# RoPE attention before two MLPs: q's rotation of five head pairs summed in PSUM, and the 1e-9 of the softmax sums on the scalar engine

## The chip, the core and the metric

The kernel runs on one core of a Trainium2 chip. The metric is the device time of one execution in microseconds (us), as a median of three runs. The engines are TensorE (PE in the profile, its weight loads PEld), VectorE (DVE), ScalarE (ACT), GpSimd (POOL) and SyncE (SP, which issues the DMAs). They run side by side, each in the order of its own queue, and wait for each other by semaphores.

## What is computed

Attention with rotary positions over 4 batches x 8 heads, 576 tokens, 64 dimensions a head; then two MLPs over the 2304 tokens (512 to 2048 to 512 each). All data is float32.

```python
def rotate(x):                       # half = 32
    x1, x2 = x[..., :half], x[..., half:]
    return concatenate([x1 * cos - x2 * sin, x1 * sin + x2 * cos], -1)
scores = rotate(q) @ rotate(k).T / sqrt(D)
scores = scores - max(scores, -1)
attn = exp(scores)
attn = attn / (sum(attn, -1) + 1e-09)
x = attn @ v                         # regrouped to 2304 x 512
h = x @ w_in;  g = where(h >= 1, h, where(h <= -1, 0, (h + 1) ** 2 / 4))
x = g @ w_out
r = maximum(x @ w_in2, 0);  out = (s * r * r + b) @ w_out2
```

## The kernel before, in words

**Pairs and units.** Two heads lie on the 128 partitions, so there are 16 pairs. A pair has nine units (`UNITS`, k = 0 to 8), 144 units in all: eight score tiles of 128 query rows, and at k = 4 a tile of the remainders. The loop over units calls five steps in the order `ORDER = "qltaf"`.

- `do_qk`: the score matmuls of a unit into one of two PSUM buffers `sc` (L307), the row maximum `nm` on DVE (L309), the exponentials `p` on ACT with their row sums (L314).
- `do_load`: the preparation of the next pairs. At k = 0 the q of pair i+1 is rotated (`rope_pair`), at k = 2 its k; at k = 4 and 6 the q and k of pair i+2 are loaded. It also issues the conversions of MLP weights (`convert`: ACT L126, four DVE instructions L127 to L130, two POOL products `wm`, two POOL sums `w`, ACT L131).
- `do_t`, two units later: transposes `tp` of `p` on PE, copied to `pt` by ACT (L333) or DVE (L335). For the last unit of each of the two groups of a pair also `inverse`, the reciprocal of the row sums: 1e-9 is added on DVE (L367, and L369 for the remainder), the reciprocal is taken on DVE (L371), and POOL spreads it to a tile `eb` (L373).
- `do_av`, four units later: the products with v (L355 to L360), the transposes `rm` of `eb` (L380), and `u = av * r` on DVE (L388 to L391).
- `do_fill`, from unit 48 on: matmuls `h` and `y` of the first MLP for batches that are finished, as filling between the attention's.

**The rotation of q before.** The host's layout holds q twice, as two planes: itself, and with its halves swapped and signed. `load_qk` loads both planes into one tile (L217, 576 KB). `rope_pair` multiplies both by the table (POOL, four instructions of 128x288; DVE for pair 1, L247) and adds them on DVE (L249, 128x576). `lay_q` then splits the sum into two fp32r parts for the two heads: for each, ACT writes the rounded part (L262, 64x576) and DVE the rest (L263, 64x576).

**What sets the order.** Within the attention no order is written out by hand: each engine's order comes from a scheduler that works with its own estimates of durations, so one edit can move instructions of all engines. The buffers are: four banks of PSUM for `tp`, `tr`, `av`, `rm`, `h`, `y` together (`bank`), two for `sc` of two banks each, four tiles for the loads of q and k, two sets of `qs`, `kh` and `kz`. Behind the attention come the two MLPs, from about 455 us to the end, in a fixed order.

Of the kernel before, what the change touches and what calls it, by code (L numbers as in the profile page):

```python
# [8 lines left out]
F32 = mybir.dt.float32  # L9
F32R = mybir.dt.float32r  # L10
# [3 lines left out]
AF = mybir.ActivationFunctionType  # L14
ALU = mybir.AluOpType
# [4 lines left out]
B, H, S, D = 4, 8, 576, 64  # L20
# [3 lines left out]
P = 128  # L24
# [28 lines left out]
N2A = 288  # L53
CAV = None
BF = 0
SPLITX = 1
N1 = 288

# [2 lines left out]
def kernel(ctx, tc, qq, kk, vv, tab, ww1, ww2, s, b, out):  # L61
    nc = tc.nc
# [6 lines left out]
    const = ctx.enter_context(tc.tile_pool(name="const", bufs=1))  # L69
    ident = const.tile([P, P], F32, name="ident")  # L70
    make_identity(nc, ident)
    s_sb = const.tile([P, 1], F32, name="s_sb")
    b_sb = const.tile([P, 1], F32, name="b_sb")

    def pool_tt(out, in0, in1, op, dim=-1):

        n = out.shape[dim]
        free = 1
        for x in out.shape[1:]:
            free *= x  # L80
        k = min(n, -(-free // PW))
        for i in range(k):
            c = [slice(None)] * len(out.shape)
            c[dim] = slice(n * i // k, n * (i + 1) // k)
            c = tuple(c)
            nc.gpsimd.tensor_tensor(out=out[c], in0=in0[c], in1=in1[c], op=op)  # L86
# [13 lines left out]
    exps = {}  # L100
# [96 lines left out]
    att = pa.enter_context(tc.tile_pool(name="att", bufs=1, side="right", reuse_waits="tile"))  # L197
    att2 = pa.enter_context(tc.tile_pool(name="att2", bufs=2, side="right", reuse_waits="tile"))
    ps_s = pp.enter_context(tc.tile_pool(name="ps_s", bufs=2, space=PSUM))
    ps_b = pp.enter_context(tc.tile_pool(name="ps_b", bufs=4 - BF, space=PSUM))  # L200
    ps_f = pp.enter_context(tc.tile_pool(name="ps_f", bufs=BF, space=PSUM)) if BF else ps_b

    tab_sb = att.tile([P, 2, S], F32, name="tab_sb")

    def bank(name):
        return ps_b.tile([P, 512], F32, tag="bank", name=name)

    qk_in, v_in, stacks = {}, {}, {}

    WHOLE = [slice(0, S)]  # L210
    HALVES = [slice(0, 288), slice(288, S)]

    def load_qk(i, nm, pieces=WHOLE):
        bb, hp = divmod(i, NP)
        t = att2.tile([P, 2, S], F32, tag="qkin", name=f"{nm}in", bufs=QB)
        for c in pieces:
            nc.sync.dma_start(out=t[:, :, c], in_=(qq if nm == "q" else kk)[bb, hp, :, :, c])  # L217
        qk_in[nm, i] = t

    def load_v(i):  # L220
        bb, hp = divmod(i, NP)
        t = att2.tile([P, 5, 2, D], F32, tag="vin", name="vin", bufs=VB)
        for out, src in ((t[:, :, 1], vv[bb, hp, :, :, 1]), (t[:D, :4, 0], vv[bb, hp, D:, :4, 0]), (t[D:, :4, 0], vv[bb, hp, :D, 1:, 0]), (t[D:, 4, 0], vv[bb, hp, :D, 0, 0])):
            nc.sync.dma_start(out=out, in_=src)
        v_in[i] = t
# [9 lines left out]
    kz_t = [att.tile([P, 2, S], F32R, name=f"kz{n}") for n in range(2)]  # L235
# [5 lines left out]
    def rope_pair(i, nm, mul, add, lo_eng, pieces=WHOLE):  # L241

        t = qk_in.pop((nm, i))
        tt = {nc.gpsimd: pool_tt, nc.vector: nc.vector.tensor_tensor}
        last = None
        for c in pieces:
            tt[mul](out=t[:, :, c], in0=t[:, :, c], in1=tab_sb[:, :, c], op=ALU.mult)  # L247
            r = t[:, 1, c]
            tt[add](out=r, in0=t[:, 0, c], in1=r, op=ALU.add)  # L249
            last = (lay_q if nm == "q" else lay_k)(i, t, c, lo_eng)  # L250
        return last

    SELF = [slice(0, D), slice(D, P)]

    def lay_q(i, t, c, lo_eng):

        st = stacks["q", i] = qs_t[i % 2]
        r = t[:, 1, c]
        for j in range(2):
            own, other = SELF[j], SELF[1 - j]  # L260
            at = slice(j * QW + c.start, j * QW + c.stop)
            nc.scalar.activation(st[own, at], r[own], AF.Copy, scale=0.125)  # L262
            nc.vector.scalar_tensor_tensor(out=st[other, at], in0=r[own], scalar=0.125, in1=st[own, at], op0=ALU.mult, op1=ALU.subtract)  # L263

    def lay_k(i, t, c, lo_engs):
        if c.start == 0:
            stacks["k", i] = att.tile([P, 2, S], F32R, tag="kh", name="kh", bufs=2), kz_t[i % 2]
        kh, kz = stacks["k", i]
        tt = {nc.gpsimd: pool_tt, nc.vector: nc.vector.tensor_tensor}
        r = t[:, 1, c]  # L270
        if i > 0:
            hi, lo = t[:, 0, c].bitcast(F32R), r.bitcast(F32R)
            nc.scalar.copy(hi, r)
            pool_tt(out=lo, in0=r, in1=t[:, 0, c], op=ALU.subtract)
            for j in range(2):
                own = SELF[j]
                for rows in SELF:
                    nc.sync.dma_start(out=kh[rows, j, c].bitcast(F32), in_=t[own, 0, c])
                m = nc.sync.dma_start(out=kz[own, j, c].bitcast(F32), in_=t[own, 1, c])
            return m.ins  # L280
        for j in range(2):
            own, other = SELF[j], SELF[1 - j]
            nc.scalar.copy(kh[own, j, c], r[own])
            m = nc.sync.dma_start(out=kh[other, j, c].bitcast(F32), in_=kh[own, j, c].bitcast(F32))
            tt[lo_engs[j]](out=kz[own, j, c], in0=r[own], in1=kh[own, j, c], op=ALU.subtract)
        return m.ins
# [6 lines left out]
    def qk(i, k):  # L293
        if k == 0:
            sums_t[i] = att2.tile([P, 9], F32, tag="sums", name="sums")
        j, t = UNITS[k]
        sc = ps_s.tile([P, 2, 512], F32, tag="sc", name="sc")
        if j is None:
            places = [(0, 512), (1, S + D)]
        else:  # L300
            places = [(j, t * P + j * (QW + D))]
        straight = [[(0, 0, 288)], [(0, 288, 288)]]
        moved = [[(0, D, 288)], [(0, 352, 224), (224, 0, D)]]
        for half in range(2):
            todo = [(stacks["q", i][:, c:c + P], r[:, h], w) for h, c in places for r in stacks["k", i] for w in (moved if j is None and h == 0 else straight)[half]]
            for m, (l, r, (o, k0, n)) in enumerate(todo):
                nc.tensor.matmul(sc[:, half, o:o + n], l, r[:, k0:k0 + n], start=m == 0, stop=m == len(todo) - 1)  # L307
        nm = att.tile([P, 1], F32, tag="nm", name="nm", bufs=4)
        nc.vector.tensor_reduce(out=nm, in_=sc[:, :, :288], axis=AX.XY, op=ALU.max, negate=True)  # L309
        if j != 1:  # L310
            p_t[i, t] = att.tile([P, 2 * S], F32, tag="p", name="p", bufs=PB)
        p = p_t[i, t][:, S * (j == 0):S * (j == 0) + S]
        col = 8 if j is None else 2 * t + j
        exps[i * 9 + k] = nc.scalar.activation(p, sc[:, :, :288], AF.Exp, bias=nm, scale=1.0, accum_out=sums_t[i][:, col:col + 1]).ins  # L314
        if j is None:
            nc.scalar.copy(p_t[i, t][:, S:S + D], p[:, 512:])
# [46 lines left out]
    def inverse(i, g):  # L363

        e = att2.tile([P, 5], F32, tag="sume", name="sume")
        sm = sums_t[i]
        nc.vector.tensor_scalar_add(e[:, 0:4], sm[:, 4 * g:4 * g + 4], 1e-9)  # L367
        if g == 0:
            nc.vector.tensor_scalar_add(e[:, 4:5], sm[:, 8:9], 1e-9)  # L369
        m = 5 - g  # L370
        nc.vector.reciprocal(e[:, :m], e[:, :m])  # L371
        eb = att2.tile([P, 4, D], F32, tag="eb", name="eb")
        nc.gpsimd.tensor_copy(eb, e[:, 0:4].unsqueeze(2).to_broadcast([P, 4, D]))  # L373
        return e, eb
# [79 lines left out]
    def convert():  # L454
        while pending:
            sl = pending.pop(0)
            if sl.made < 2:
                sl.half(wst, WB)
                break
# [20 lines left out]
    def do_load(n):  # L480
        if n < len(units):
            i, k = units[n]
            if i + 1 < NPAIR:
                if k == 0:
                    rope_pair(i + 1, "q", nc.gpsimd if i else nc.vector, nc.vector, None)
                elif k == 2:
                    rope_pair(i + 1, "k", nc.gpsimd, nc.gpsimd, [nc.gpsimd, nc.vector])
                elif k == 3:
                    load_v(i + 1)
                elif k in (4, 6) and i + 2 < NPAIR:  # L490
                    load_qk(i + 2, "q" if k == 4 else "k")

        if n in range(33, 51, 2) or n in range(70, 110, 4):
            with tc.issue_after(exps[n - 14]):
                convert()
# [124 lines left out]
    last = FC * N1  # L620
# [57 lines left out]
```

## Time and profile before

| | us |
|---|---|
| median of 3 runs (1163.46 to 1164.19) | 1163.69 |
| the profiled execution, its own time | 1162.87 |
| its span in the profile | 1161.1 |
| PE busy in the span | 1100.2 (95%) |
| DVE busy | 610.5 (53%) |
| ACT busy | 690.8 (59%) |
| POOL busy | 563.6 (49%) |

The profiled execution is 0.82 us under the median, and 1.8 us of it lie outside its span. Busy shares are means over stages with different limits: up to about 143 us only attention runs, from there to about 455 us attention with the first MLP's matmuls between it, then the MLPs alone. So the rows below are read stage by stage: 14.7 us is the first row maximum, 77.3 that of the fourth pair, 143.6 that of unit 53. A "row" of a view that groups instructions gives the line in the code, the engine, the operation, output and inputs with their shapes, the count, then busy us and the mean ns of one, then the idle time of that engine ahead of them and what ended it.

### The profile page before, as it was taken

The numbers are of one execution on the slowest core, as the hardware profiler recorded it, in microseconds if no ns is written. First come the engines' busy times: TensorE is split into PE (matmuls) and PEld (weight loads), VectorE is DVE, ScalarE is ACT, GpSimd is POOL, SyncE is SP. The second block draws the span as 40 slices with busy tenths as digits, with TensorE's granted clock in tenths as the row PEclk, the third lists the DMA queues.
The fourth block names the chain that finished last, engine by engine and source line by source line (L and its number), as shares of the span: only waits on it lengthen the run. The fifth ranks groups of instructions, "written<-read, shape, count | busy, mean of one in ns | idle before, by whom it ended". The sixth has DMA issues, their size and how long they took to land.

```text
span 1161.1 us, 18714 instructions
## 1 busy us (share of the span) xinstructions
PE 1100.2 (95%) x6720; PEld 993.9 (86%) x6720; DVE 610.5 (53%) x1030; ACT 690.8 (59%) x1450; POOL 563.6 (49%) x748
## 2 busy tenths in 40 slices
PE   4887899899999999999999899999999999999998
PEld 4666688789888988998999899998888889988887
DVE  6988789786655553666655566654411111221221
ACT  4666666766666665566555455477755645555443
POOL 6987787884441101666688896556610110111000
PEclk9998899899999999999999999999999999999999
DMA  7754555654443312434345453435211210311220
GB/s 210 210 166 144 149 156 167 183 154 142 122 119 94 100 35 72 129 125 139 94 148 156 149 177 123 140 112 165 75 45 54 66 52 15 98 46 62 66 66 33
DMA packets 86749, 132.37 MB, mean 114 GB/s; under 512 B 28672, under 2 KB 66816, under 8 KB 86656
## 3 DMA queue, kind: packets, MB, share of 16 engines
q1 hardware_dynamic: 86656, 131.17, 37.7%
q8 instruction: 53, 0.87, 0.3%
q14 instruction: 40, 0.33, 0.1%
HBM read 91.03 MB, written 26.54 MB: 101 GB/s over the span
## 4 chain that ended last, share of the span: by engine, by line
PE 63%; POOL 11%; DVE 9%; issue 5%; DMA 5%; ACT 5%; SPq 1%; POOLq 0%; ACTq 0%; DVEq 0%
PE hps L144 22%; PE yps L592 7%; PE yps L593 7%; PE yps L591 7%; PE sc L307 4%; PE h L144 4%; PE y L144 3%; PE av L355 3%; PE tp L329 3%; POOL kin L86 3%; DMA xs<-xd 2%; POOL wm L86 2%; POOL w L86 2%; POOL xl L86 2%; DVE nm L309 2%
## 5 line engine op out<-in xcount | busy, mean ns | idle before, releaser
L144 PE MATMUL hps<-xh,w 128*128 128x464 f32 (+5 forms) x1216 | 344.8, 349 | 0.0
L86 POOL TENSOR_TENSOR xl<-xs,xh 128x232 fp32r<-128x232 f32 (+5 forms) x172 | 132.7, 795 | 273.0 <-ACT xh L90 272.3
L144 PEld LDWEIGHTS hps<-xh,w 128*128 128x128 f32 x1216 | 222.0, 188 | 15.1
L591 PE MATMUL yps<-gh,w 128*128 128x464 f32 (+5 forms) x608 | 213.9, 352 | 5.4 <-ACT yo L598 5.1
L592 PE MATMUL yps<-gl,w 128*128 128x464 f32 (+5 forms) x608 | 213.3, 351 | 3.2 <-DVE gl L94 3.2
L593 PE MATMUL yps<-gh,w 128*128 128x464 f32 (+5 forms) x608 | 213.0, 350 | 0.0
L144 PE MATMUL hps<-xl,w 128*128 128x464 f32 (+5 forms) x608 | 211.7, 348 | 0.2 <-POOL xl L86 0.2
L94 DVE TENSOR_TENSOR gl<-ar,gh 128x464 fp32r<-128x464 f32 (+1 forms) x80 | 57.3, 716 | 267.0 <-ACT gh L90 266.9
L86 POOL TENSOR_TENSOR wm<-wm,w 128x256 f32<-128x256 f32 x128 | 112.7, 901 | 106.7 <-ACT w L131 55.6
L307 PE MATMUL sc<-kh,qs 128*128 128x288 f32 x336 | 105.8, 336 | 43.0 <-ACT p L314 29.6
L309 DVE TENSOR_REDUCE nm<-sc 128x1 f32<-128x576 f32 x144 | 106.8, 752 | 54.1 <-PE sc L307 53.1
L591 PEld LDWEIGHTS yps<-gh,w 128*128 128x128 f32 x608 | 114.9, 189 | 15.4 <-ACT yo L598 6.9
L592 PEld LDWEIGHTS yps<-gl,w 128*128 128x128 f32 x608 | 115.2, 189 | 11.5 <-DVE gl L94 3.9
L314 ACT ACTIVATE p<-sc,nm 128x576 f32<-128x576 f32 x144 | 106.6, 743 | 27.7 <-DVE nm L309 26.8
L593 PEld LDWEIGHTS yps<-gh,w 128*128 128x128 f32 x608 | 115.3, 190 | 7.5
L175 ACT ACTIVATE ar<-hps 128x464 f32<-128x464 f32 (+1 forms) x80 | 44.3, 554 | 129.6 <-PE hps L144 129.5
L144 PEld LDWEIGHTS hps<-xl,w 128*128 128x128 f32 x608 | 114.4, 188 | 8.1 <-POOL xl L86 0.5
L307 PEld LDWEIGHTS sc<-kh,qs 128*128 128x128 f32 x336 | 66.5, 201 | 53.5 <-ACT p L314 38.3
L86 POOL TENSOR_TENSOR w<-wm,wa 128x256 fp32r<-128x256 f32 x128 | 101.0, 806 | 0.0
L307 PE MATMUL sc<-kz,qs 128*128 128x288 f32 x336 | 97.0, 308 | 0.1
L94 DVE TENSOR_TENSOR gl<-ac,gh 128x288 fp32r<-128x288 f32 (+3 forms) x112 | 79.7, 712 | 32.9 <-ACT gh L90 32.9
L329 PE MATMUL tp<-ident,p 128*128 128x128 f32 x576 | 91.8, 284 | 0.0
(81 smaller groups left out, 1989.9 us busy)
## 6 DMA issues: line engine op xcount, KB each, us to landing
wraw<-in_ww SPq DMA_DIRECT2D x64, 512.0 KB, 3.7
kin<-in_k SPq DMA_DIRECT2D x15, 576.0 KB, 4.7
qin<-in_q SPq DMA_DIRECT2D x15, 576.0 KB, 4.0
kh<-kin SPq DMA_DIRECT2D x60, 144.0 KB, 2.6
xs<-y1d SPq DMA_DIRECT2D x32, 232.0 KB, 2.5
xs<-xd SPq DMA_DIRECT2D x44, 144.0 KB, 2.4
yd<-ys SPq DMA_DIRECT2D x40, 144.0 KB, 2.2
xd<-u SPq DMA_DIRECT2D x16, 288.0 KB, 2.4
```

Of the source, the lines that this page charges most:

```text
L86: nc.gpsimd.tensor_tensor(out=out[c], in0=in0[c], in1=in1[c], op=op)
L94: tt(out=dst_lo, in0=src, in1=dst_hi, op=ALU.subtract)
L144: m = nc.tensor.matmul(out_ps, l, r, start=(i == 0), stop=(i == n - 1))
L175: nc.scalar.activation(r, h, AF.Relu)
L307: nc.tensor.matmul(sc[:, half, o:o + n], l, r[:, k0:k0 + n], start=m == 0, stop=m == len(todo) - 1)
L309: nc.vector.tensor_reduce(out=nm, in_=sc[:, :, :288], axis=AX.XY, op=ALU.max, negate=True)
L314: exps[i * 9 + k] = nc.scalar.activation(p, sc[:, :, :288], AF.Exp, bias=nm, scale=1.0, accum_out=sums_t[i][:, col:col + 1]).ins
L329: nc.tensor.transpose(v[:, c, :], p[:, c * P:(c + 1) * P], ident)
L355: nc.tensor.matmul(ps[j * D:(j + 1) * D, :n], v[:, kt, j, :], pt[g][:, kt, j, :], start=kt == 0, stop=False)
L591: nc.tensor.matmul(acc, wh, gh, start=f == 0, stop=False)
L592: nc.tensor.matmul(acc, wh, gl, start=False, stop=False)
L593: nc.tensor.matmul(acc, wl, gh, start=False, stop=last)
```

## The change

For pairs 1 to 5 (`ON_PE`, `NR`):

- q is loaded once (one plane, 288 KB instead of 576 KB).
- At k = 0 `rope_mul` makes two products from that one plane, with the cosines and with the sines. They have the same sizes as before.
- At k = 3 (`AFTER`) `rope_sum` forms the sum on PE: for each half of the 576 columns, a PSUM bank `ro` takes ident times the cosine product plus `turn` times the sine product. `turn` is the identity with its halves swapped and signed, made once at the start by two DVE instructions. They are float32 matmuls of 128x288, four for each pair, 20 in all.
- `lay_q` reads the sum from PSUM, half by half: four ACT and four DVE instructions of 64x288 in the place of two and two of 64x576.

For all 16 pairs the 1e-9 is added by one ACT instruction for each group (128x5 or 128x4, bias `eps`), 32 in all, in the place of 48 on DVE (L367 and L369). The columns of the sums are renumbered for that. `stack_k` is a part of `lay_k` under a name of its own; k is treated as before. Pairs 0 and 6 to 15 rotate q as before.

```diff
+ON_PE = ('q',)
+NR = 6
+AFTER = 3
...
+    eps = const.tile([P, 1], F32, name="eps")
+    nc.vector.memset(eps, 1e-9)
...
+    turn = att.tile([P, P], F32, name="turn")
+    for n in range(2):
+        nc.vector.tensor_scalar(out=turn.rearrange("p (a t w) -> p a t w", t=2, w=D // 2)[:, :, n, :], in0=ident.rearrange("p (a t w) -> p a t w", t=2, w=D // 2)[:, :, 1 - n, :], scalar1=-1.0, scalar2=None, op0=ALU.mult)
...
     def load_qk(i, nm, pieces=WHOLE):
...
+        if nm in ON_PE and 0 < i < NR:
+            nc.sync.dma_start(out=t[:, 0], in_=(qq if nm == "q" else kk)[bb, hp, :, 0, :])
+            qk_in[nm, i] = t
+            return
...
+    def rope_mul(i, nm, eng):
+        t = qk_in[nm, i]
+        tt = pool_tt if eng is nc.gpsimd else nc.vector.tensor_tensor
+        for n in (1, 0):
+            tt(out=t[:, n], in0=t[:, 0], in1=tab_sb[:, n], op=ALU.mult)
+
+    def rope_sum(i, nm):
+        t = qk_in.pop((nm, i))
+        for c in HALVES:
+            ps = bank("ro")[:, :288]
+            nc.tensor.matmul(ps, ident, t[:, 0, c], start=True, stop=False)
+            nc.tensor.matmul(ps, turn, t[:, 1, c], start=False, stop=True)
+            if nm == "q":
+                lay_q(i, ps, c)
...
-    def lay_q(i, t, c, lo_eng):
+    def lay_q(i, r, c):
         st = stacks["q", i] = qs_t[i % 2]
-        r = t[:, 1, c]
...
-        col = 8 if j is None else 2 * t + j
+        col = 4 if j is None else 2 * t + j + t // 2
...
-        nc.vector.tensor_scalar_add(e[:, 0:4], sm[:, 4 * g:4 * g + 4], 1e-9)
-        if g == 0:
-            nc.vector.tensor_scalar_add(e[:, 4:5], sm[:, 8:9], 1e-9)
         m = 5 - g
+        nc.scalar.activation(e[:, :m], sm[:, 5 * g:5 * g + m], AF.Identity, bias=eps, scale=1.0)
         nc.vector.reciprocal(e[:, :m], e[:, :m])
...
-                if k == 0:
-                    rope_pair(i + 1, "q", nc.gpsimd if i else nc.vector, nc.vector, None)
-                elif k == 2:
-                    rope_pair(i + 1, "k", nc.gpsimd, nc.gpsimd, [nc.gpsimd, nc.vector])
-                elif k == 3:
+                for nm, at, eng in (("q", 0, nc.gpsimd if i else nc.vector), ("k", 2, nc.gpsimd)):
+                    if nm not in ON_PE or i + 1 >= NR:
+                        if k == at:
+                            rope_pair(i + 1, nm, eng, nc.vector if nm == "q" else nc.gpsimd, [nc.gpsimd, nc.vector])
+                    elif k == at:
+                        rope_mul(i + 1, nm, eng)
+                    elif k == at + AFTER:
+                        with tc.issue_after(exps[n - 4]) if n >= 4 else ExitStack():
+                            rope_sum(i + 1, nm)
```

The scheduler orders the engines anew. Three places show it; a row is line, operation, output and inputs, shape, and a count. The names with numbers (`qs_103`, `qs_108`, `kz_...`) are the buffers of q and k.

VectorE before, in pair 2 (the third), behind the row maximum of unit 21 (k = 3) and up to those of units 22 and 23:

```order
L309 TENSOR_REDUCE nm<-sc 128x1
L128 SCALAR_TENSOR_TENSOR wm<-wa,wm 128x512
L335 COPY pt<-tp 128x4x128
L129 TENSOR_SCALAR wa<-wm 128x512
L367 TENSOR_SCALAR sume<-sums 128x4
L249 TENSOR_TENSOR qin<-qin 128x576
L130 SCALAR_TENSOR_TENSOR wa<-wraw,wa 128x512
L388 TENSOR_TENSOR u<-av,r 128x256
L309 TENSOR_REDUCE nm<-sc 128x1 x2
L335 COPY pt<-tp 128x4x128
```

VectorE after, at the same place, from the row maximum of unit 20 to that of unit 22:

```order
L347 TENSOR_REDUCE nm<-sc 128x1
L132 TENSOR_SCALAR wm<-wa 128x512
L133 SCALAR_TENSOR_TENSOR wm<-wa,wm 128x512
L134 TENSOR_SCALAR wa<-wm 128x512
L306 SCALAR_TENSOR_TENSOR qs_108<-ro,qs_108 64x288
L135 SCALAR_TENSOR_TENSOR wa<-wraw,wa 128x512
L347 TENSOR_REDUCE nm<-sc 128x1
L306 SCALAR_TENSOR_TENSOR qs_108<-ro,qs_108 64x288
L373 COPY pt<-tp 128x4x128
L306 SCALAR_TENSOR_TENSOR qs_108<-ro,qs_108 64x288 x2
L132 TENSOR_SCALAR wm<-wa 128x512
L347 TENSOR_REDUCE nm<-sc 128x1
```

Between two row maxima the 1e-9 (L367) and the sum of q (L249) are gone; the four instructions on `ro` have come in, and a conversion (L132 to L135) stands a unit earlier. Counted along the whole order, the conversions that are complete ahead of unit 53 are 6 before and 9 now.

TensorE before, in pair 1, units 11 and 12, ahead of the products with v:

```order
L329 MATMUL tp<-ident,p 128x128 x4
L307 MATMUL sc<-kh,qs_103 128x288
L307 MATMUL sc<-kz_105,qs_103 128x288
L307 MATMUL sc<-kh,qs_103 128x288
L307 MATMUL sc<-kz_105,qs_103 128x288
L329 MATMUL tp<-ident,p 128x128 x4
L355 MATMUL av<-pt,vin 64x256 x8
```

TensorE after, at the same place:

```order
L345 MATMUL sc<-kz_110,qs_108 128x288
L367 MATMUL tp<-ident,p 128x128 x4
L277 MATMUL ro<-qin,ident 128x288
L278 MATMUL ro<-qin,turn 128x288
L277 MATMUL ro<-qin,ident 128x288
L278 MATMUL ro<-qin,turn 128x288
L345 MATMUL sc<-kh,qs_108 128x288
```

The four matmuls into two `ro` banks stand between the transposes of one unit and the scores of the next. The transposes `rm`, which before came at once behind the products with v, stand behind the scores of unit 13 now (in pairs 2 and 3 behind those of two units).

GpSimd before, around the first two `eb` (the two groups of pair 0):

```order
L86 TENSOR_TENSOR qin<-qin,tab_sb 128x2x144 x4
L86 TENSOR_TENSOR kin<-kin,tab_sb 128x2x144 x4
L373 COPY eb<-sume 128x256
L86 TENSOR_TENSOR kin<-kin 128x288 x2
L373 COPY eb<-sume 128x256
```

GpSimd after, at the same place:

```order
L91 TENSOR_TENSOR qin<-qin,tab_sb 128x288 x2
L91 TENSOR_TENSOR kin<-kin 128x288
L409 COPY eb<-sume 128x256
L91 TENSOR_TENSOR kin<-kin 128x288
L91 TENSOR_TENSOR qin<-qin,tab_sb 128x288 x2
L91 TENSOR_TENSOR kin<-kin,tab_sb 128x2x144 x4
L409 COPY eb<-sume 128x256
```

Ahead of the second `eb` now stand the four products of pair 3's k and two of its q's, which came behind it before. Counted to the third `eb`, six instructions on k more stand ahead of it (28, before 22).

## Rows read from the trace of the kernel before

**Rows 1.** Windows by stage: length, then busy us by engine, granted clock, DMA:

```profile
core 0: us, PE busy (x) PEld busy (x) DVE busy (x) ACT busy (x) POOL busy (x), PEclk, DMA share, GB/s
14.70:77.30 62.60, 53.06 (x370) 42.95 (x370) 54.79 (x87) 41.51 (x92) 56.10 (x72) 1.00 0.72 200
77.30:143.60 66.30, 54.03 (x365) 43.26 (x364) 55.56 (x96) 41.90 (x96) 52.66 (x70) 0.87 0.53 156
143.60:270.00 126.40, 116.44 (x868) 100.02 (x867) 107.05 (x186) 86.66 (x206) 93.19 (x118) 0.97 0.57 170
270.00:455.00 185.00, 181.58 (x1422) 162.50 (x1421) 106.94 (x212) 115.16 (x289) 49.16 (x74) 1.00 0.31 87
455.00:1161.10 706.10, 693.70 (x3700) 643.75 (x3697) 278.06 (x442) 400.76 (x760) 305.31 (x396) 1.00 0.32 98
```

**Rows 2.** Waits, 14.7 to 143.6 us: who waited for whom, us, times, longest:

```profile
PE sc L307 <- ACT p L314: 21.7, 22, 2.7
DVE nm L309 <- PE sc L307: 10.9, 17, 1.9
```

**Rows 3.** VectorE groups, 14.7 to 143.6 us: busy us, mean ns | idle before:

```profile
L309 DVE TENSOR_REDUCE nm<-sc 128x1 f32<-128x576 f32 x54 | 40.1, 752 | 11.3 <-PE sc L307 10.9
...
L263 DVE SCALAR_TENSOR_TENSOR qs<-qin,qs 64x576 fp32r<-64x576 f32 x13 | 13.0, 1004 | 0.5 <-ACT qs L262 0.2
L249 DVE TENSOR_TENSOR qin<-qin 128x576 f32<-128x576 f32 x8 | 9.8, 1219 | 0.5 <-POOL qin L86 0.5
L367 DVE TENSOR_SCALAR sume<-sums 128x4 f32<-128x4 f32 x11 | 6.6, 602 | 0.5 <-ACT p L314 0.3
L130 DVE SCALAR_TENSOR_TENSOR wa<-wraw,wa 128x512 f32<-128x512 uint16 x6 | 5.6, 936 | 0.0
L128 DVE SCALAR_TENSOR_TENSOR wm<-wa,wm 128x512 uint32<-128x512 uint32 x6 | 4.2, 700 | 0.1
L127 DVE TENSOR_SCALAR wm<-wa 128x512 uint32<-128x512 uint32 x6 | 4.2, 694 | 2.5 <-ACT wa L126 2.4
...
L129 DVE TENSOR_SCALAR wa<-wm 128x512 uint32<-128x512 uint32 x6 | 3.1, 514 | 0.1
```

**Rows 4.** GpSimd groups, 14.7 to 143.6 us:

```profile
L86 POOL TENSOR_TENSOR kin<-kin,tab_sb 128x288 f32<-128x288 f32 x32 | 30.5, 982 | 4.7 <-DMA kin<-in_k 3.8 <-DMA xs<-xd 0.7
...
L86 POOL TENSOR_TENSOR w<-wm,wa 128x256 fp32r<-128x256 f32 x12 | 10.0, 858 | 0.0
L86 POOL TENSOR_TENSOR wm<-wm,w 128x256 f32<-128x256 f32 x12 | 9.0, 771 | 1.3 <-DVE sume L371 1.3
```

**Rows 5.** GpSimd timeline, the third `eb`: start us, us, what:

```profile
49.94 0.61 POOL L373 COPY eb<-sume 128x256 f32<-128x256 f32 x1
```

**Rows 6.** TensorE timeline: products with v, `rm` of that `eb`, a wait:

```profile
51.05 2.37 PE L355 MATMUL av<-pt,vin 128*64 128x320 f32 x16
...
53.91 0.44 PE L380 MATMUL rm<-ident,eb 128*128 128x128 f32 x2
...
136.20 0.40 PE L307 MATMUL sc<-kh,qs 128*128 128x288 f32 x1 [2.66 <-ACT p L314]
```

**Rows 7.** Window in the second stage with a lower granted clock:

```profile
137.00:144.00 7.00, 6.23 (x30) 5.80 (x27) 3.23 (x5) 5.23 (x12) 5.16 (x9) 0.51 0.32 97
```

**Rows 8.** VectorE groups, 143.6 to 270 us:

```profile
L367 DVE TENSOR_SCALAR sume<-sums 128x4 f32<-128x4 f32 x9 | 3.5, 390 | 0.2
```

**Rows 9.** Waits, 143.6 to 270 us:

```profile
PE sc L307 <- ACT p L314: 5.7, 6, 2.2
```

**Rows 10.** VectorE reading PSUM, one line: count, then ns min/median/max:

```profile
L167 DVE SCALAR_TENSOR_TENSOR ac<-h,ac x40: 442/450/459, 154.8 to 453.9; 128x288 f32<-128x288 f32 x40
```

**Rows 11.** ScalarE reading PSUM, 128x288, the same view:

```profile
L165 ACT ACTIVATE ac<-h x40: 396/412/433, 153.7 to 452.8; 128x288 f32<-128x288 f32 x40
```

**Rows 12.** ScalarE groups, 14.7 to 143.6 us:

```profile
L314 ACT ACTIVATION_READ_ACCUMULATOR p<-sc,nm 128x1 f32 x53 | 10.5, 199 | 0.0
L262 ACT ACTIVATE qs<-qin 64x576 fp32r<-64x576 f32 x14 | 9.5, 682 | 1.6 <-PE sc L307 1.5
```

More of the change, by code (lines that the diff above doesn't have):

```diff
@@ L249, in rope_pair, with stack_k @@
             tt[add](out=r, in0=t[:, 0, c], in1=r, op=ALU.add)
-            last = (lay_q if nm == "q" else lay_k)(i, t, c, lo_eng)
+            last = lay_q(i, r, c) if nm == "q" else lay_k(i, t, c, lo_eng)
         return last
+    def rope_mul(i, nm, eng):
[11 more added lines that the diff above has]
+                lay_q(i, ps, c)
+            else:
+                hi, lo = t[:, 0, c].bitcast(F32R), t[:, 1, c].bitcast(F32R)
+                nc.scalar.copy(hi, ps)
+                nc.vector.tensor_tensor(out=lo, in0=ps, in1=t[:, 0, c], op=ALU.subtract)
+        if nm == "k":
+            stack_k(i, t, WHOLE[0])
+    def stack_k(i, t, c):
+        kh, kz = stacks["k", i] = att.tile([P, 2, S], F32R, tag="kh", name="kh", bufs=2), kz_t[i % 2]
+        for j in range(2):
+            own = SELF[j]
+            for rows in SELF:
+                nc.sync.dma_start(out=kh[rows, j, c].bitcast(F32), in_=t[own, 0, c])
+            m = nc.sync.dma_start(out=kz[own, j, c].bitcast(F32), in_=t[own, 1, c])
+        return m.ins
     SELF = [slice(0, D), slice(D, P)]
-    def lay_q(i, t, c, lo_eng):
+    def lay_q(i, r, c):
         st = stacks["q", i] = qs_t[i % 2]
-        r = t[:, 1, c]
         for j in range(2):
@@ L265, in lay_k @@
     def lay_k(i, t, c, lo_engs):
-        if c.start == 0:
+        if i == 0 and c.start == 0:
             stacks["k", i] = att.tile([P, 2, S], F32R, tag="kh", name="kh", bufs=2), kz_t[i % 2]
-        kh, kz = stacks["k", i]
         tt = {nc.gpsimd: pool_tt, nc.vector: nc.vector.tensor_tensor}
@@ L274, in lay_k @@
             pool_tt(out=lo, in0=r, in1=t[:, 0, c], op=ALU.subtract)
[L275 to L280, printed above, removed]
+            return stack_k(i, t, c)
+        kh, kz = stacks["k", i]
         for j in range(2):
@@ L483, in do_load @@
             if i + 1 < NPAIR:
-                if k == 0:
-                    rope_pair(i + 1, "q", nc.gpsimd if i else nc.vector, nc.vector, None)
-                elif k == 2:
-                    rope_pair(i + 1, "k", nc.gpsimd, nc.gpsimd, [nc.gpsimd, nc.vector])
-                elif k == 3:
+                for nm, at, eng in (("q", 0, nc.gpsimd if i else nc.vector), ("k", 2, nc.gpsimd)):
[7 more added lines that the diff above has]
+                            rope_sum(i + 1, nm)
+                if k == 3:
                     load_v(i + 1)
```

## The prediction

> **What bounds the kernel now.** I read the windows by stage first, since the busy shares of the whole span mean nothing here. Behind 455 us the tensor engine is busy 693.70 of 706.10 us, and from 270 to 455 us 181.58 of 185 [rows 1]. Nothing that the change takes from VectorE can be gained there. The 126.4 us from 143.6 to 270 leave TensorE 10.0 us idle (126.40 - 116.44), and the 128.9 us before them 21.8 (9.5 and 12.3 in the two windows). So the gain is bounded by some 32 us, plus what a low clock costs: in the second window the granted clock is 0.87 on the mean, and from 137 to 144 us 0.51, about the 1.2 GHz level, behind a wait of TensorE of 2.66 us [rows 1, 6, 7].
>
> Then the waits. From 14.7 to 143.6 us TensorE's scores wait 21.7 us in 22 waits for ACT's exponentials (a `sc` buffer has to come free), and those wait for VectorE's row maximum. But VectorE itself waits 10.9 us for scores [rows 2]. So it is a ring, scores, maximum, exponential, in which VectorE is late at some units and early at others. Its groups show with what it is filled: 40.1 us are the maxima, the rest is work that stands between them [rows 3].
>
> The last reading is the one that tempers the forecast: in 14.7 to 77.3 us **POOL** is the fullest, 56.10 of 62.60 us, before DVE with 54.79 and TensorE with 53.06 [rows 1]. All three are over 84% busy there, so an edit that relieves one of them meets the next at once.
>
> **The change part by part.** *Sum of q.* Five additions go from DVE; at the group's mean of 1.22 us that is 6.1 us [rows 3]. The order has all five ahead of the maximum of unit 22, so they lie in the first window.
>
> *Layout of q.* Ten instructions of 1.00 us become twenty that read PSUM. Nearest is the 128x288 combination from PSUM with 0.45 us and hardly any spread [rows 10]: 20 x 0.45 = 9.0 against 10.0, so -1.0 on DVE (0 if a half costs half of what it does now). On ACT ten of 0.68 become twenty of about 0.41 [rows 11, 12]: +1.4 us over five pairs, beside an ACT engine with over 20 us idle in either window.
>
> *1e-9.* In 14.7 to 143.6 us eleven L367 of 0.60 go, 6.6 us, and six L369 with them, which no row here prices; the nearest is L367's later mean of 0.39, so at most 2.3 more, and I take 0.8. In 143.6 to 270 it is 3.5 us [rows 3, 8] plus 0.5. ACT gets 32 instructions of at most five columns. Between the 0.20 us of the 128x1 accumulator read and the 0.41 us of a 128x288 activation [rows 11, 12] I take 0.3, nearer the small one: 20 x 0.3 = 6 us up to 270 us. ACT has room in sum, but one of them ahead of an exponential delays the ring by itself: I put **+1 us** on the path, bounds 0 and 20 x 0.41 = 8.
>
> A rule speaks against this edit. The page "ScalarE: Activation LUTs" of the Trainium skill, section "Rules for kernel authors", gives additions to VectorE, not ScalarE. Its own price for an activation with a pointer as bias (section "What ACT_TABLE_LOAD costs", 280 ns and 0.83 ns a column) makes an estimate of 0.28 us for five columns. The trace has 0.60 us for the same addition on VectorE in the first stage, so here the row, not the rule, decides; by the page's price the 20 would be 5.7 us of ACT, the same +1 on the path.
>
> *Matmuls of the sum.* The trace has no float32 matmul of full width with 288 columns. Nearest are the products with v: eight instructions of 64 columns width in 2.37 us, 0.30 each [rows 6]. If a full one costs the same, 20 x 0.27 = 5.3 us for 288 columns; if two halves run side by side there, twice that, 10.7. Either is 1 to 2 us for each of five pairs on an engine with 9.5 us idle in the first window. I put **+0.5** on the path, bounds 0 and 10.7.
>
> The page "FP8 and Floating Point Precision", section "TensorE Precision Notes", says that a true float32 matmul takes four passes. That gives an estimate of 4 x 288 / 2.4 GHz = 0.48 us each, 9.6 us in all, near the upper of the two ends; the 0.30 us of a 320-column one agree with that only if its halves overlap. The sum would be the same, as long as the idle time covers it.
>
> *Conversions.* This is not in the diff, only in the order: nine instead of six conversions are complete ahead of unit 53. One costs DVE 0.94 + 0.70 + 0.69 + 0.51 = 2.84 us [rows 3] and POOL 2 x 0.86 + 2 x 0.77 = 3.26 [rows 4]. So 8.5 us of DVE work and 9.8 us of POOL work move from behind 143.6 us to ahead of it. By the count of the order about half of it falls on either window.
>
> *POOL's order.* Ahead of the third `eb` stand six instructions on k more, at 0.98 us 5.9 us [rows 4]. That `eb` began at 49.94 and its transposes ran at 53.91 [rows 5, 6], a slack of 3.4 us behind its own 0.61. Moved whole it is late by 2.5 us, and TensorE waits in order at that place, unless the smaller loads let POOL run faster.
>
> **The sum by windows.**
> - 14.7 to 77.3 us: DVE -6.1 - 0.8 (layout) - 4.0 (half of the 1e-9) + 4.3 (half of the conversions) = -6.6 of 54.79. POOL gets 4.9 us more with 6.5 idle, and the late `eb`. Taken: **-1.5**, bounds -5 and +3.
> - 77.3 to 143.6: DVE -3.4 - 0.2 + 4.2 = about 0. Taken: **0**, bounds -5 (the low clock gone) and +3.
> - 143.6 to 270: DVE -8.5 - 4.0 = -12.5 of 107.05, POOL -9.8. TensorE's idle 10.0 us is the cap, of which 5.7 are waits for exponentials [rows 9]. Taken: **-4.5**, bounds 0 and -10.
> - Behind 270: 0.
> - ACT's new instructions +1, the matmuls +0.5.
>
> Together -4.5 us: the profiled execution's 1162.87 would be 1158.4, the median, which lies 0.82 above it, **1159.2 us**.
>
> The other edits cost nothing here: `turn` and `eps` are made while VectorE waits for the first loads, and the halved loads take work from DMA engines that are 72% busy in the first window [rows 1]. POOL is what uses q, and it is too full to start much earlier.
>
> **The rivals.** *(a) Nothing arrives.* VectorE's time turns into waits for scores, of which it has 10.9 us already [rows 2], and the earlier conversions take the rest of POOL. For: three engines over 84%. Against: the third stage loses 12.5 us of DVE work with no new work for it. It gives -1 or so, 1162.7.
>
> *(b) The clock holds.* The stretch at the low level follows a long wait of TensorE, 2.66 us at 136.20 [rows 6, 7]. If the shorter queue of VectorE keeps these waits short, the second window is no longer at 0.87: 13% of 54.03 us of busy time, of which half or more can be had, 4 to 7 us. It gives 1159.2 - 6 = 1153. Against: that window's DVE work does not shrink.
>
> *(c) Slower: the banks.* The four banks serve `tp`, `tr`, `av`, `rm` and now two `ro`, which are held until DVE has done the last of four splits; these stand behind a maximum and a copy in its order. If TensorE, in order, comes to an allocation before that, it waits, five times. At the price of the long wait in the trace, 2.66 us [rows 6], that is 13.3 - 4.5 = +8.8: 1172.5. It decides from 0.9 us for each pair on (0.9 x 5 = 4.5). Against: two banks remain, and behind `ro` come scores, which need none, and only then one `tp` and one `av`. With a mean of 1.5 us it would be 1166.7, which I take as its value.
>
> That the change does not do what it says is excluded by the order: twenty matmuls on `ro`, loads of 128x576, no L367 or L369.
>
> **How the numbers follow.** The forecast, between -8 and -2.3 us, gets 0.48; (a) 0.20; (b) and others beyond -8 us 0.14; (c) and a late `eb` 0.18. A measurement tells 0.2%, 2.3 us, from no change. So faster 0.62, same 0.20, slower 0.18. For 8 in 10 I leave out the lower half of (b) and the upper half of (c): **1152 to 1166**; the forecast's own range is 1155.7 to 1161.4.
>
> **What would show it.** The L249 and L263 rows in the first window fall by 5 and 8, and twenty rows near 0.45 us appear on `ro`; anything over 0.6 fails that step. The ACT add should be at 0.25 to 0.35. DVE's busy time ahead of unit 53 should fall by about 6 to 7 us, and by 12 behind it up to 270 us; the row maximum of unit 53 should come at about 142 us (143.6 now), the end of the fills near 450.5. If the gain lies ahead of unit 53, POOL was no bound; a POOL idle time under 3 us in the first 60 us would say that it was. A wait of TensorE for `qs` on DVE at `rm` or `tp`, five times, would be (c). The forecast is wrong if the third stage keeps its 10 us of idle TensorE.

## The result, and the profile after

The changed kernel takes 1177.32 us in the median of four runs (1174.72 to 1180.26), against 1163.94 in the four of before: a ratio of 1.0112, with a 95% interval of 1.0088 to 1.0137. It is slower by some 13 us, where -4.5 was forecast. The profiled execution took 1174.72 us, the lowest of the four, so its trace shows somewhat less than the loss of the medians: the span grew by 11.8 us (1172.9 from 1161.1).

The windows of the changed kernel answer to [rows 1]; the borders are the same row maxima as there (the first, that of the fourth pair, that of unit 53), then 270 us. Columns: from and to, length, busy us of TensorE, its weight loads, VectorE, ScalarE and GpSimd (the count of instructions in brackets), granted clock, DMA share, GB/s.

```profile
14.90:83.00 68.10, 58.65 (x390) 46.55 (x390) 47.58 (x84) 43.96 (x105) 56.03 (x78) 0.95 0.61 171
83.00:154.80 71.80, 59.23 (x402) 47.04 (x402) 60.24 (x99) 47.15 (x111) 55.63 (x74) 0.90 0.53 153
154.80:270.00 115.20, 104.72 (x794) 91.15 (x791) 93.09 (x151) 78.41 (x192) 85.23 (x107) 0.97 0.55 161
```

The first stretch took 62.6 us and takes 68.1, the second 66.3 and now 71.8. From there to the end it is 1017.5 us before (1161.1 - 143.6) and 1018.1 now. So the loss lies ahead of unit 53, 5.5 us in each half, and the gain forecast behind it did not come. VectorE has less to do in the first stretch (47.58 us for 54.79), and the stretch is longer all the same, so its busy time was not what bounded it. Over both stretches VectorE's work fell by 2.5 us only (110.35 to 107.82), where the prediction's terms make 6.6: the conversions in them, nine for six, took longer than was put (3.12 us each for 2.84).

What the change itself adds came out as sized. VectorE's and ScalarE's groups, 14.9 to 154.8 us (count, busy us, mean ns, idle before, its releaser):

```profile
L306 DVE SCALAR_TENSOR_TENSOR qs<-ro,qs 64x288 fp32r<-64x288 f32 x20 | 8.8, 454 | 4.3 <-ACT qs L305 3.9
L133 DVE SCALAR_TENSOR_TENSOR wm<-wa,wm 128x512 uint32<-128x512 uint32 x9 | 8.0, 884 | 0.2
...
L132 DVE TENSOR_SCALAR wm<-wa 128x512 uint32<-128x512 uint32 x9 | 7.0, 779 | 5.8 <-ACT wa L131 5.7
```

```profile
L305 ACT ACTIVATE qs<-ro 64x288 fp32r<-64x288 f32 x20 | 8.0, 404 | 3.6 <-DVE qs L306 3.4
L131 ACT ACTIVATE wa<-wraw 128x512 f32<-128x512 f32 x9 | 6.0, 667 | 8.7 <-POOL w L91 8.7
...
L406 ACT ACTIVATE sume<-sums,eps 128x5 f32<-128x5 f32 x6 | 1.8, 304 | 0.0
```

The splits from PSUM take 0.454 and 0.404 us, the 1e-9 on ScalarE 0.30. What is new stands in the last column: ScalarE sat idle 8.7 us ahead of the first instruction of a conversion (L131), for GpSimd's `w`, and VectorE 5.7 us for that instruction. The waits of the same stretch (who waited for whom, us, times, longest), after and then, for three of them, before (14.7 to 143.6 us):

```profile
PE sc L345 <- ACT p L352: 21.1, 18, 3.4
POOL qin L91 <- DMA qin<-in_q: 19.9, 5, 8.0
DVE nm L347 <- PE sc L345: 16.5, 17, 2.2
ACT p L352 <- DVE nm L347: 10.0, 17, 1.8
ACT wa L131 <- POOL w L91: 8.7, 5, 3.9
...
PEld rm L416 <- POOL eb L409: 0.4, 1, 0.4
...
PEld tp L367 <- DVE qs L306: 0.2, 1, 0.2
```

```profile
POOL qin L86 <- DMA qin<-in_q: 8.7, 3, 4.4
...
DVE wm L127 <- ACT wa L126: 2.4, 2, 1.3
...
ACT wa L126 <- POOL w L86: 2.0, 1, 2.0
```

TensorE's waits for exponentials are as long in sum as before (21.7 [rows 2]) but longer one by one, and VectorE waits 16.5 us for scores where it was 10.9.

**Where it happens.** Pair 2 shows it best: from its first row maximum to that of pair 3 it takes 26.6 us, where it was 21.8. These are rows of the timelines (start, us, engine, line and what it does, in brackets the idle time before it and what ended it). GpSimd:

```profile
61.44 3.71 POOL L91 TENSOR_TENSOR qin<-qin,tab_sb 128x288 f32<-128x288 f32 x4 [3.36 <-DMA qin<-in_q]
65.10 1.44 POOL L91 TENSOR_TENSOR wm<-wm,w 128x256 f32<-128x256 f32 x2
66.49 1.43 POOL L91 TENSOR_TENSOR w<-wm,wa 128x256 fp32r<-128x256 f32 x2
```

ScalarE:

```profile
67.94 0.67 ACT L131 ACTIVATE wa<-wraw 128x512 f32<-128x512 f32 x1 [2.24 <-POOL w L91]
...
70.52 0.74 ACT L352 ACTIVATE p<-sc,nm 128x576 f32<-128x576 f32 x1 [1.51 <-DVE nm L347]
```

VectorE:

```profile
68.64 1.05 DVE L132 TENSOR_SCALAR wm<-wa 128x512 uint32<-128x512 uint32 x1 [2.17 <-ACT wa L131]
69.72 0.76 DVE L347 TENSOR_REDUCE nm<-sc 128x1 f32<-128x576 f32 x1
```

TensorE, and the window behind that wait:

```profile
71.40 0.40 PE L345 MATMUL sc<-kh,qs 128*128 128x288 f32 x1 [3.36 <-ACT p L352]
...
74.04 0.61 PE L345 MATMUL sc<-kh,qs 128*128 128x288 f32 x1 [1.08 <-ACT p L352]
```

```profile
74.00:82.00 8.00, 7.96 (x41) 5.51 (x42) 5.95 (x12) 4.79 (x11) 6.06 (x9) 0.61 0.69 188
```

Read in order of time it is one chain through four engines. GpSimd waits for the load of a q until 61.44, multiplies it, and only then does the products and sums of the first conversion, which end at 67.92. The next conversion needs the same buffer `wa` (there is one), so ScalarE's L131 waits for that; VectorE's L132 waits for L131; and the row maximum of unit 22 is queued right behind L132, though its scores are there. TensorE waits 3.36 us for the exponential behind that maximum. Then the granted clock is 0.61 over eight microseconds, and TensorE is busy for 7.96 of them. The order ahead of the prediction has this very row: L132 between the last splits of `ro` and the maximum. Behind 113 us the chain comes once more, as far as ScalarE: GpSimd's product of q (after 7.97 us of waiting for its load), `wm`, `w`, ScalarE's `wa`. There it reaches the ring on ScalarE itself. The maximum was done at 119.25, but the exponential is queued behind that `wa` and a copy:

```profile
119.97 0.67 ACT L131 ACTIVATE wa<-wraw 128x512 f32<-128x512 f32 x1 [3.85 <-POOL w L91]
120.66 0.37 ACT L421 COPY r<-rm 128x256 f32<-128x256 f32 x1
120.93 0.75 ACT L352 ACTIVATE p<-sc,nm 128x576 f32<-128x576 f32 x1
```

### The profile page after: what moved, and what is told of

It reads as the page before. It is cut to its first block, busy times and chain, and to the rows that moved or that the text cites. A ratio compares the mean times of both kernels' runs of the same rounds, so it can differ in the third digit from the quotient of the medians.

```text
span 1172.9 us, 18798 instructions
## 1 busy us (share of the span) xinstructions
PE 1107.8 (94%) x6760; PEld 999.2 (85%) x6760; DVE 600.8 (51%) x991; ACT 698.9 (60%) x1492; POOL 560.0 (48%) x748
## 4 chain that ended last, share of the span: by engine, by line
PE 56%; POOL 13%; DMA 9%; DVE 9%; ACT 6%; issue 5%; SPq 1%; POOLq 0%; ACTq 0%; DVEq 0%
PE hps L149 20%; PE yps L633 7%; PE yps L634 7%; PE yps L632 7%; PE sc L345 4%; DMA xs<-xd 3%; POOL wm L91 3%; POOL w L91 3%; PE av L393 3%; PE h L149 3%; POOL xl L91 3%; PE y L149 2%; PE tp L367 2%; POOL kin L91 2%; ACT p L352 1%
## 5 line engine op out<-in xcount | busy, mean ns | idle before, releaser
L367 PE MATMUL tp<-ident,p 128*128 128x128 f32 x576 | 90.7, 282 | 0.4 <-ACT r L421 0.4
```

The costliest lines, as they stand in the source:

```text
L367: nc.tensor.transpose(v[:, c, :], p[:, c * P:(c + 1) * P], ident)
```

## The experiments

The runs are called e1 to e12 in the order in which they stand here. Ratios are against the kernel before on the same chip, with 95% intervals; its medians there were 1163.7 to 1164.5 us. I call the account above the *conversions theory*. Its rivals are that the sum in PSUM costs time by itself, and that the 1e-9 on ScalarE does.

**One part alone.** First only the 1e-9:

```diff
-ON_PE = ('q',)
+ON_PE = ()
```

> Only the 1e-9 on the scalar engine; q is rotated as before in all pairs. Conversions theory (the loss comes from weight conversions that the scheduler pulls ahead, which tie the row maxima to ScalarE and ScalarE to GpSimd's last sums of a conversion): the order has 6 conversions complete ahead of unit 53, as before, so 1160 to 1165 us. Scalar-engine theory (the added instructions delay the exponentials): 1168 us or more, with unit 53 some 5 us later than 143.6.

1162.36 us, ratio 0.9981 (0.9964 to 0.9998). By itself the 1e-9 on ScalarE is no loss; it is a gain of some 2 us, with an interval that ends near zero. The number of conversions ahead of unit 53 stays as before with it. Then only the sum of q:

```diff
-        nc.scalar.activation(e[:, :m], sm[:, 5 * g:5 * g + m], AF.Identity, bias=eps, scale=1.0)
+        nc.vector.tensor_scalar_add(e[:, 0:4], sm[:, 5 * g:5 * g + 4], 1e-9)
+        if g == 0:
+            nc.vector.tensor_scalar_add(e[:, 4:5], sm[:, 4:5], 1e-9)
```

> Only q's sum in PSUM for pairs 1 to 5; the 1e-9 stays on VectorE. The order has 8 conversions complete ahead of unit 53. Conversions theory and PSUM-sum theory (the matmuls of 2 us a pair and the four and four splits that wait for each other cost about 2 us a pair by themselves): both 1170 to 1178 us, unit 53 at 150 to 155. Scalar-engine theory: 1160 to 1166.

1172.75 us, 1.0087 (1.0059 to 1.0115). Most of the loss comes with the sum of q, whether by itself or by what the scheduler does around it. The two parts do not simply add: beside the sum of q the 1e-9 took the ratio from 1.0087 to 1.0112, with one conversion more ahead of unit 53 (9 for 8), though these two intervals overlap.

**The conversions held back.**

```diff
-            with tc.issue_after(exps[n - 14]):
+            with tc.issue_after(exps[n - 8]):
                 convert()
```

> The whole change, but a conversion may start only behind the exponential of 8 units before its place instead of 14; the order has 6 complete ahead of unit 53, as before the change. Conversions theory: the loss ahead of unit 53 (11 us) mostly goes, unit 53 at 141 to 147, 1160 to 1167 us. PSUM-sum theory: unit 53 stays at 150 or later, 1172 or more.

1164.23 us, 1.0008 (0.9993 to 1.0024): the loss is gone with the sum in PSUM untouched, and unit 53 comes at 145.0 us in its trace (154.8 with the change, 143.6 before). No gain has come in its place; the 1e-9 alone is some 2 us faster (0.9981). In its order the first conversion is complete behind the maximum of unit 26 (before: unit 21), and between 32 and 118 us its trace has no wait of TensorE over 1.1 us. ScalarE's waits for `w` are down to

```profile
ACT wa L131 <- POOL w L91: 2.0, 2, 1.2
```

**The buffer.** If the single `wa` is the link, a second pair of buffers should cut it. In the first trial every other *half* of a slice got it, and since the first halves of four slices come in a row, the first four conversions all used the old one:

```diff
...
-            a = stage.tile([P, HW], F32, tag="wa", name="wa", bufs=bufs)
...
+            spare = alt if alt is not None and self.made == 2 else stage
+            a = spare.tile([P, HW], F32, tag="wa", name="wa", bufs=bufs)
...
```

> The whole change, with a second pair of buffers (wa, wm) for every other conversion during the attention, so that ScalarE's first instruction of a conversion need not wait for GpSimd's last of the one before. The conversions stay early (9 ahead of unit 53). Conversions theory: ScalarE's waits for w on GpSimd, 8.6 us ahead of 160 us, fall under 3, unit 53 at 145 to 150, 1165 to 1171 us. PSUM-sum theory: no change, 1174 or more.

1178.65 us, 1.0131 (1.0101 to 1.0162). The trial did not test the link: the wait at the place in question stood, with 3.00 us. The next one alternates from the first conversion on (the edit against the trial just before):

```diff
-            spare = alt if alt is not None and self.made == 2 else stage
+            turns.append(0)
+            spare = alt if alt is not None and len(turns) % 2 == 0 else stage
```

> The whole change, conversions alternating between two pairs of buffers (wa, wm) from the first on; in the run before, the second pair was first used by the fifth conversion, so the wait at 66 us stood. Conversions are early (9 ahead of unit 53, all nine ahead of unit 41). If the loss is ScalarE's wait for GpSimd's w behind the late product of q: those waits under 2 us up to 100 us, pair 2 back at 21 to 23 us from its first row maximum to that of pair 3 (26.6 after the change), 1164 to 1170 us. If it is the conversions' work itself ahead of the maxima: pair 2 still at 25 or more, 1172 or more.

1170.83 us, 1.0056 (1.0038 to 1.0075): half of the loss is gone. Its trace has, from 14.7 to 155 us, of the 8.7 us only

```profile
ACT wa L134 <- POOL w L91: 0.5, 2, 0.3
```

So the second pair of buffers cuts these waits, and the time falls by 6.5 us. That the waits at `wa` are worth those 6.5 us is not shown. Pair 2 still took 26.7 us with the wait gone, as the other half of the expectation said, and unit 53 came at 154.4 us, as with the change; the profiled execution was the slowest of its six (1173.54). The freed conversions come still more closely, all nine ahead of unit 41, four of them in pair 2.

**Pair by pair.** The traces of all the runs with the sum in PSUM say more than the totals. This table is the time of pairs 1 to 4, from a pair's first row maximum to the next pair's; a conversion counts where its last VectorE instruction stands, and the waits are those of ScalarE's `wa` for GpSimd's `w`.

| conversions in the pair | pairs, us |
|---|---|
| 0 | 19.9 to 21.2 (all of e8, pair 1 of the others, pair 2 of e11) |
| 1 | 20.8 (e3), 20.9 (e12) |
| 2, no wait over 0.2 us | 21.9 (e3), 23.9 (e2), 24.9 (e5), 25.1 (e2), 25.5 (e4) |
| 2, with a wait of 0.9 to 3.9 us | 24.1 (e3), 24.8 (the change), 26.1 (e4), 26.6 (the change), 26.6 (e11), 27.1 (e11) |
| 3 or 4, no wait over 0.4 us | 26.7, 27.9 (both e5) |
| 3 or 4, with a wait of 1.0 to 3.0 us | 26.6 (the change), 26.7 (e2), 27.0 (e12), 27.5 (e12), 27.8 (e4) |

All these pairs hold the four matmuls of a sum of q, and e8, further down, is the change without its early conversions. Such a pair takes 20 to 21 us when it holds no conversion or one, and some 27 when it holds three or four, whether or not ScalarE waited for the buffer; with two, those with a wait are the longer ones in the mean. This points to the crowding of conversions as what costs, and to the buffer as a part of that at most. The runs of the kernel before do not order in this way: in the one without early conversions these four pairs took from 18.9 to 23.5 us.

**Early conversions without the change.** The kernel before, with its conversions allowed earlier:

```diff
-            with tc.issue_after(exps[n - 14]):
+            with tc.issue_after(exps[max(n - 24, 0)]):
```

> The kernel before, its conversions allowed 24 units ahead of their place instead of 14: the order has 7 complete ahead of unit 53 (before 6), and 3 ahead of unit 30 (before 2). No other edit. If early conversions cost time by themselves, 1165 to 1170 us with the loss in pairs 1 and 2; if they cost only beside the sum in PSUM, 1161 to 1165.

1170.39 us, 1.0053 (1.0028 to 1.0078). One more conversion ahead of unit 53, and the others earlier, cost 6 us with nothing else edited. Its profiled execution was the lowest of its runs (1166.05), so its trace does not show where the rest lies; in it pair 1, which now holds a conversion, takes 23.1 us for 19.9, and pair 4 20.9 for 23.2.

**No early conversions at all.** In both kernels the first nine are replaced by a memset:

```diff
+            if len(out9) < 9:
+                out9.append(0)
+                nc.gpsimd.memset(self.w[:, :, k:k + HW].bitcast(F32), 0.0)
+                return
```

> The kernel before, its first nine conversions left out (a GpSimd memset in the place of load, four DVE, two ScalarE and four GpSimd instructions each); the MLP weights of those nine half slices are zero. 1140 to 1155 us; unit 53 at 125 to 135 us.

> The changed kernel with the same nine conversions left out in the same way. Conversions theory: against e7 between -6 and +1 us, since the saved 15 us of DVE work ahead of unit 53 are then really free. PSUM-sum theory (the matmuls, the held banks, the splits that wait for ScalarE): +6 to +12 against e7.

1153.62 us, 0.9921 (0.9893 to 0.9949), for the kernel before; 1157.19, 0.9940 (0.9918 to 0.9962), for the changed one. The change costs 3.6 us by these medians and 2.2 by the ratios, whose intervals overlap. That lies between the two expectations: it is far from 13, but the sum in PSUM may keep a price of its own of a few us. The other way round, the nine conversions cost 0.8% of 1164 us, 9 us, in the kernel before, and 1.0112 - 0.9940 = 1.7%, 20 us, in the changed one. And the change gains nothing even here. The stretch from the first row maximum to that of unit 53, of the kernel before and then of the changed one, without conversions (the third busy time is VectorE's):

```profile
19.80:140.60 120.80, 101.41 (x732) 80.93 (x733) 91.14 (x156) 77.54 (x176) 81.34 (x116) 0.96 0.52 146
```

```profile
19.00:139.60 120.60, 107.01 (x773) 85.68 (x774) 77.59 (x145) 80.85 (x198) 77.96 (x117) 1.00 0.50 137
```

VectorE has 13.6 us less to do, and the stretch is as long. The profiled execution of the first was the slowest of its runs (1160.03 us), so its stretch is rather shorter in the others. Unit 53 came at 140.6 us in it, later than the 125 to 135 that were expected, also because the first row maximum came at 19.8 (14.7 in the kernel before). The work that the change takes from VectorE is worth next to nothing on this path.

**Later still.** Would conversions that come later make either kernel faster? The places moved by four units in the kernel with only the 1e-9 and in the kernel before, and by eight (`range(41, 59, 2)`) in the changed one:

```diff
-        if n in range(33, 51, 2) or n in range(70, 110, 4):
+        if n in range(37, 55, 2) or n in range(70, 110, 4):
```

> The 1e-9 on the scalar engine alone, and the nine conversions' places four units later: the order has 5 complete ahead of unit 53, none ahead of unit 27. If early conversions cost time in the stage without filling work, 1158 to 1162 us, faster than the 1e-9 alone (1162.4); if the matmuls that fill the gaps then wait for weights, 1163 or more.

> The kernel before with the same later places and no other edit: 5 conversions complete ahead of unit 53. Early-conversions theory: 1159 to 1164 us; the difference to e9 is the price of the 1e-9 on either engine, 0 to 2 us.

> The whole change with the conversions' places eight units later: 6 complete ahead of unit 53, none ahead of unit 31. Conversions theory: 1158 to 1165 us, as e3 (1164.2) or better; unit 53 at 140 to 145. PSUM-sum theory: 1168 or more.

1163.44 us, 0.9989 (0.9974 to 1.0004); 1166.75, 1.0023 (1.0008 to 1.0039); 1170.52, 1.0059 (1.0038 to 1.0080). Later is not better, and all three miss what the account of early conversions expected: the first lies where the rival put it, the second above its range. In the kernel before, earlier and later places both cost (6 and 3 us), so that the order was moved at all may be a part of the loss. The third lies where the PSUM-sum theory put it: it has 6 conversions ahead of unit 53, as e3, and is 6 us slower. So their number ahead of a unit is not the measure. Its trace speaks for crowding, not for the sum: pairs 0 to 2, without conversions, take 20.4 to 20.5 us each; pairs 3 and 4, with two each, 26.6 and 27.1, and in each the chain of before 70 us stands again. ScalarE and TensorE in these pairs, and the window behind each:

```profile
89.09 0.67 ACT L131 ACTIVATE wa<-wraw 128x512 f32<-128x512 f32 x1 [1.07 <-POOL w L91]
```

```profile
114.66 0.68 ACT L131 ACTIVATE wa<-wraw 128x512 f32<-128x512 f32 x1 [3.15 <-POOL w L91]
```

```profile
92.55 0.57 PE L345 MATMUL sc<-kh,qs 128*128 128x288 f32 x1 [3.32 <-ACT p L352]
```

```profile
119.40 0.40 PE L345 MATMUL sc<-kh,qs 128*128 128x288 f32 x1 [4.16 <-ACT p L352]
```

```profile
92.50:99.50 7.00, 6.18 (x26) 5.74 (x27) 5.38 (x11) 5.12 (x13) 6.43 (x10) 0.51 0.25 68
99.50:119.40 19.90, 15.52 (x117) 11.76 (x115) 15.76 (x27) 11.07 (x28) 11.45 (x16) 1.00 0.57 164
119.40:127.00 7.60, 6.83 (x31) 5.91 (x33) 5.30 (x10) 6.21 (x15) 6.62 (x10) 0.55 0.44 139
```

Each time a wait of 3 to 4 us, and then half the clock for 7. It is again the second of two conversions that waits, for sums of the first that stand behind GpSimd's product of a q. The trace of e3 has no such wait up to 118 us.

**Both edits together**, `exps[n - 8]` as in e3 and the alternating buffers as in e5:

> The whole change with both edits: conversions allowed 8 units ahead of their place (as in e3) and alternating between two pairs of buffers (as in e5). The order has 9 complete ahead of unit 53, the first behind unit 26, eight of them between units 30 and 49. If the number of conversions in that stage costs by itself, as in e5: 1167 to 1172 us, slower than e3 (1164.2) although ScalarE's waits for GpSimd's w are gone; if only those waits cost: 1160 to 1165.

1168.95 us, 1.0031 (1.0012 to 1.0049). It is 5 us slower than e3, as was expected if the number of conversions in this stage costs; the two intervals overlap a little. Nine conversions stand ahead of unit 53 again in the place of six, seven of them in pairs 3 and 4, which take 27.0 and 27.5 us. It is no clean price of their number: ScalarE's waits for `w` are not gone (2.8 us), and the transposes wait for the splits of `ro`, the mechanism of the prediction's rival (c), once for 1.9 us (1.3 us in e5):

```profile
PE tp L371 <- DVE qs L310: 2.5, 2, 1.9
```

What the runs show together: the loss comes and goes with where the scheduler puts the conversions (e3, e6, and e8 against e7). How much of it each link of a crowded pair costs, the buffer, the work ahead of the maxima or the clock, they do not separate. The kernel before with `exps[n - 8]`, the control to e3, was not run.

## Why the prediction was wrong

- **The reading of the bound was half right.** That relief of one engine need not come through was said, and it did not. But it was put down to full engines, and in the longer stretch that came none is fuller than TensorE with 58.65 of 68.10 us; what the rows show instead are waits between queues. And the sum credited VectorE's 6.6 us in the first window with a gain of 1.5, and 12.5 in the third with 4.5. Without conversions 13.6 us less of VectorE's work gained nothing (e8 against e7), and unit 53 to the end took 1018.1 us for 1017.5. VectorE's busy time was not a bound in either.
- **The step that failed is "Conversions".** I saw in the order that three more stand ahead of unit 53, priced them at 2.84 us of VectorE and 3.26 of GpSimd, and treated both as work that fills idle time, "about half of it on either window". In the trace a conversion is a chain, ScalarE, VectorE, ScalarE, GpSimd, with one buffer, and its instructions stand ahead of maxima and exponentials in queues that run in order. A pair with three of them took 26.6 us or more where a pair with none took 20 to 21, and holding them back alone took the change from 1.0112 to 1.0008. The first window was put at -1.5 and measured +5.5, the second at 0 and measured +5.5. Both bounds of +3 were too narrow. Even as busy time it was too small: the four instructions took 0.78 + 0.88 + 0.64 + 0.82 = 3.12 us. Nor did half of the three fall on either window: two stand ahead of 83.0 us and one behind.
- **The third window**, -4.5, did not show in the total. TensorE is idle for 10.5 of the 115.2 us up to 270, the sign that the prediction named for this.
- **Layout of q**: 0.454 us on VectorE, 0.404 on ScalarE, as put. **1e-9**: 0.30 us, as put; its +1 on the path was not measured by itself: the whole edit, with the work that it takes from VectorE, gains some 2 us alone. **Matmuls**: each of the twenty stands as two rows in the trace; four in a row start 0.49 us apart, near the upper end of the bounds. That agrees with the four passes of the Trainium skill, page "FP8 and Floating Point Precision", section "TensorE Precision Notes", and the estimate of 0.48 us made from it. The rows of the first and last of these four and of the scores behind them, on TensorE:

```profile
59.59 0.65 PE L277 MATMUL ro<-qin,ident 128*128 128x288 f32 x2
...
61.05 0.65 PE L278 MATMUL ro<-qin,turn 128*128 128x288 f32 x2
61.32 0.51 PE L345 MATMUL sc<-kh,qs 128*128 128x288 f32 x1
```

- **The rivals.** The median lies beyond the value of (c), 1166.7, but its mechanism did not occur in the changed kernel: in 14.9 to 154.8 us TensorE waited 0.2 us for the splits of `ro`. In (a) stood what was seen, VectorE's waits for scores growing (10.9 us became 16.5) and the earlier conversions, but with no price for either. The clock, rival (b), did not help: 1.00 became 0.95 in the first stretch, 0.87 became 0.90 in the second.
- **GpSimd** was named as the fullest engine, with a late `eb` as its effect. The late `eb` cost 0.4 us. GpSimd did hold the chain, but by another path: its `w`, behind a product of q that waited for its load (19.9 us of such waits for 8.7 before).

What stays open: how the loss divides among the links of a crowded pair; where the 6.5 us lie that the second buffers gave back; why the kernel before with earlier conversions (e6) loses 6 us in most runs while its trace, of a quick execution, shows half of that; and how much of the 2 to 4 us between e7 and e8 is the sum in PSUM itself. That GpSimd's wait for q's load is what makes `w` late was read from the chain and not tried.

## What to carry to other kernels

When an edit frees an engine in a kernel whose order a scheduler makes, look first at what the scheduler pulls into the gap, and at each instruction that now stands directly ahead of one on the critical ring: which engine does it wait for, and what is queued there. A step that runs through several engines is not priced by its busy times as filling: here three or four of them in one pair went with 6 to 7 us more, and a single one with under 1 us. And test an engine as the bound before selling its time: taking 13.6 us of VectorE's work out of a stretch in which it had 91.1 gained nothing.

## What the runs showed of the hardware

In the changed kernel and in e11 a wait of TensorE of 3.3 to 4.2 us was followed each time by 7 to 8 us at a granted clock of 0.51 to 0.61. The matmuls of the same 128x288 scores then take 0.44 us for 0.29 and start 0.24 us apart for 0.13; the changed kernel, on either side:

```profile
71.77 0.29 PE L345 MATMUL sc<-kh,qs 128*128 128x288 f32 x1
71.90 0.29 PE L345 MATMUL sc<-kz,qs 128*128 128x288 f32 x1
...
74.44 0.44 PE L345 MATMUL sc<-kz,qs 128*128 128x288 f32 x1
74.68 0.44 PE L345 MATMUL sc<-kh,qs 128*128 128x288 f32 x1
```

At 0.51 a window of 7 us has 3.4 us of full speed less, so by an estimate from these rows a stall of 3 us costs about 6 where TensorE is busy behind it. That was to be seen in the rows of before, but I had counted it only as something to be gained. Shorter waits went either way: 2.21 us at 127.8 us in e3 was followed by ten us at 1.00, and 1.49 us at 111.5 in the kernel before by 6.8 us at 0.50 from 113.3 on.

The clock column can't be read ahead of 20 to 28 us. It says 1.00 there, but up to 27 us in the kernel before, and up to 19 in the changed one, the same scores take 0.44 us, as they do at 0.51 later. Of the kernel before:

```profile
21.96 0.44 PE L307 MATMUL sc<-kz,qs 128*128 128x288 f32 x1
```
